# Two gates' rows by transposes, a sum and a round trip through DRAM instead of products with ones

## The chip, the cores and the metric

The kernel runs on one core of a Trainium2 chip. The core has a matrix engine (TensorE, "PE" in the profile, with its weight loads as "PEld"), a vector engine (VectorE, "DVE"), an activation engine (ScalarE, "ACT"), a general engine (GpSimd, "POOL") and SyncE ("SP"), which here only issues transfers. Sixteen DMA engines carry the transfers that SP, ACT and POOL issue. PE writes to eight PSUM banks; ACT and DVE read them.

The metric is the device time of one execution in microseconds. Three runs of the kernel before took 773.56 to 774.21 us, with a median of 773.87.

## The reference

One transformer block for 2048 tokens of width 640, all in float32. A condition vector `c` modulates it: six rows of 640 come from one product, and two of them, `ga` and `gb`, are the gates that this case is about.

```python
mod = (_silu(c) @ w_mod).reshape(c.shape[0], 6, 1, -1)
sa, ca, ga, sb, cb, gb = (mod[:, 0], mod[:, 1], ..., mod[:, 5])
h = _layernorm(x) * (1 + ca) + sa
x = x + ga * _A_ref(h, A_wqkv, A_w_phi, A_wo)     # linear attention, 32 heads of 20
h = _layernorm(x) * (1 + cb) + sb
x = x + gb * _B_ref(h, B_w1, B_b1, B_w2, B_b2)    # two layers, relu squared, width 1728
```

In `_A_ref`, q and k pass a product per head and two softmaxes, one of the values and one of the negated values; the features then give `num / den` of linear attention, and `wo` projects the result.

A gate is a row along the feature axis, and the kernel needs it spread over all 128 partitions: `ga` is multiplied into `wo` when the weights are prepared, `gb` into the second layer's results and its bias.

## The kernel before, in words

**Tiles.** Tokens are cut into 16 tiles of 128 (`NT`); x is loaded in pairs of tiles (`XB[j]`, j = 0 to 7). The 640 features are cut into five chunks of 128 (`NC`). Every weight and activation is split into a high and a low part, and a product is three matmuls (`three`). Most matmuls come from one line, L77 in `mm`, so the profile tells them apart by the tile that they write: `pk`, `pq`, `pv` for the projections, `kvp` for keys times values, `pwo` for the output projection, `up` and `acc` for the two layers.

**The modulation.** The rows `sa` and `ca` (parts 0 and 1) are made at the start. For parts 2 to 5, `mod_mac` and `gb_mac` load a piece of `w_mod` of 128 rows (`stage`, on SP) and accumulate it on DVE, each partition with its own entry of silu(c) (`mac`, L293 and L295). What is left in `MA[part]` is 128 partial rows, which must be summed over the partitions. There are two ways in the code:

- Parts 3 and 4, which are needed as columns: `mod_turn` transposes chunks of `MA` on PE (L304) into a PSUM bank, ACT copies them into a row `mt` (L305), and `mod_sum` sums along the free axis on DVE (L309). Four chunks go together after a `do_kv`, the fifth rides in the bank of a LayerNorm transpose, in `t1(..., more=...)`.
- Parts 2 and 5, the gates, which are needed as rows on all partitions: `mod_row` multiplies by a 128 x 128 matrix of ones on PE (L327), 320 columns at a time, and ACT copies the result into `ga_b` or `gb_b` (L328).

**Phase 1** (L711 to L758) goes over the tiles t = 2 to 13: the key projection, the value projection, `do_kv` for the two tiles before (at even t), the LayerNorm of a coming pair of x tiles (`ln_parts`, in three parts: the sums, the squares, the scaling), then the query projection with the transposes `t1` of the next pair within it. PE's order is written out by hand. DVE, ACT, POOL and SP are ordered by the planner, which simulates the work with its own costs and keeps the order of the code as priority; `tc.issue_after(x)` adds that an instruction comes behind x on its engine, and `newest(engine)` is the last one written so far. The LayerNorm of the last pair (j = 7) has its sums and squares at t = 11 (`NT - 5`), the sums behind the copy of that tile's key projection.

`SIDE[t]` at the end of a tile holds the modulation's accumulation and the preparation of `wo` (`prep_wo`: load, times `ga_b` at L498, split); `AFTER_KV[t]` stands behind `do_kv`, and `LAST_COL[t]` says which part's fifth chunk rides along.

**Phase 2** starts at L761. There PE, DVE, ACT and POOL have a hand-written order, and SP is still the planner's. The last keys and values are done, `kv_diags` turns the sums of keys times values (`kvt`, L834 and L835), and `num(j)`, `num_hi(j)`, `num_lo(j)` make the numerators: products `numa`, `numb`, `numc`, copies of their high part by ACT (L942), a product with a negated unit matrix that leaves the low part (L948), and its copy (L951). `tr_e` transposes the scaled query features (`te`, copied to `ept`). Then a loop over j = 0 to 7 does the output projection (`do_wo`) and the next pair's transposes and numerators. At j = 5 it makes `bb`, the gated bias, from `gb_b` (L1139).

**Phase 3** from L1506 on is the two layers.

**Buffers.** A tile has a tag, and a tag has so many buffers: the rows `s1` have five (pieces of `w_mod`, the turned rows `mt`, raw `wo`, raw weights of the layers); the PSUM tag `tp` has one bank and serves `t1`, `mod_turn` and `mod_row` in phase 1; the projections' tag `pj` has four; the banks of phase 2 (`bank`) are three. Whoever wants a buffer waits until all readers of its previous tile are done.

Of the kernel before, what the change touches and what calls it, by code (L numbers as in the profile page):

```python
# [15 lines left out]
P = 128  # L16
# [34 lines left out]
def kernel(  # L51
# [85 lines left out]
    def tp(name):  # L137
        return psA.tile([P, 512], F32, tag="tp", name=name)
# [160 lines left out]
    def mod_turn(part, p, *cs_):  # L299
        t = MT.setdefault(part, None) or row("s1", f"mt{part}")  # L300
        MT[part] = t
        a, n = cs_[0] * P, len(cs_) * P
        for i, c in enumerate(cs_):
            nc.tensor.transpose(p[:, i * P : (i + 1) * P], MA[part][:, c * P : (c + 1) * P], ident)  # L304
        nc.scalar.activation(t[:, a : a + n], p[:, :n], AF.Copy)  # L305
# [12 lines left out]
    def mod_mac(part, *ks):  # L318
        for k, t in [(k, stage(part * D, k)) for k in ks]:
            with tc.issue_after(newest(ET_.DVE)):  # L320
                mac(t, t, k, MA.get(part))
            MA[part] = t

    def mod_row(part, dest, h, p=None):
        p = p or tp(f"mr{part}_{h}")
        c = slice(h * HALF, (h + 1) * HALF)
        nc.tensor.matmul(p[:, :HALF], ones, MA[part][:, c], start=True, stop=True)  # L327
        nc.scalar.activation(dest[:, c], p[:, :HALF], AF.Copy)  # L328

    def ln_parts(xt, nm, spare=None):  # L330
        sm = small([P, 2], "sm", f"sm{nm}")
# [45 lines left out]
    def newest(engine):  # L377
        return next(i for i in reversed(nc.cur_bb.bb.instructions) if i.engine == engine)
# [55 lines left out]
    def exps(e):  # L434
        nc.scalar.activation(e[:, 0], e[:, 0], AF.Exp)  # L435
        nc.scalar.activation(e[:, 1], e[:, 1], AF.Exp, scale=-1.0)  # L436
# [86 lines left out]
    def wo_weights(*gs):  # L523
# [1 line left out]
            prep_wo(g, ga_b)  # L525

    AFTER_KV = {
        6: lambda: mod_turn(3, tp("mc3"), 0, 1, 2, 3),
        8: lambda: mod_row(2, ga_b, 0),
        10: lambda: mod_turn(4, tp("mc4"), 0, 1, 2, 3),  # L530
        12: lambda: t1(NT // 2 - 1, 2, 3),
    }
    LAST_COL = {7: (3, cols_b[:, 0:5]), 11: (4, cols_b[:, 5:10])}
    SIDE = {
        2: lambda: mod_mac(3, 0, 1, 2),
        3: lambda: (mod_mac(3, 3, 4), mod_mac(4, 0)),
        4: lambda: mod_mac(4, 1, 2),
        5: lambda: (mod_mac(4, 3, 4), mod_mac(2, 0)),
        6: lambda: mod_mac(2, 1, 2, 3),
        7: lambda: mod_mac(2, 4),  # L540
        8: lambda: None,
        9: lambda: wo_weights(0, 1),
        10: lambda: wo_weights(2),
        11: lambda: None,
# [166 lines left out]
    for t in range(2, NT - 2):  # L711
        j, i = divmod(t, 2)
        if i == 0 and j < NT // 2 - 2:
            load_x(j + 2)
        PK[t] = row("s2", f"k{t}")
        to_sb(proj("k", t), PK[t])
        if t == NT - 4:
            t1(j + 1, 0, 1)
        if t == 9:
            mod_row(2, ga_b, 1)  # L720
        norm = j + 1 if i == 0 and t < NT - 4 else j + 2 if t == NT - 5 else None
        if norm:
            parts = ln_parts(XB[norm], f"a{norm}")
            with tc.issue_after(newest(ET_.Activation)):
                next(parts)
        p = proj("v", t, (1, 0, lambda: t1(j + 1, 4)) if t == NT - 3 else None)
        if i == 0:
            do_kv(t - 2)
            do_kv(t - 1)
            if t in AFTER_KV:  # L730
                AFTER_KV[t]()
        v_out(t, p)
        if norm:
            next(parts)
        EK[t] = tok2("k", f"ek{t}")
        spread(PK[t], EK[t], f"k{t}")
        exps(EK[t])
        if norm and not i:
            next(parts)
        if i and t < NT - 4:  # L740
            t1(j + 1, 2, 3)
        with tc.issue_after(newest(ET_.DVE)):
            k_norm(EK[t], t)
        if t < NT - POSTPONED:
            do_q(t, (1, 3, lambda: t1(j + 1, 4, more=LAST_COL.get(t))) if i else None)
            if norm and i:
                with tc.issue_after(newest(ET_.Activation)), tc.issue_after(DONE[0]):
                    next(parts)
            if i:
                with tc.issue_after(DONE[1]):  # L750
                    q_chain(t)
            else:
                q_chain(t)
        if i == 0 and t < NT - 4:
            t1(j + 1, 0, 1)
        SIDE[t]()
    pe.__exit__(None, None, None)
    behind.close()  # L758
# [40 lines left out]
    def bank(nm):  # L799
        return psB.tile([P, 512], F32, tag="m", name=nm)  # L800
# [30 lines left out]
    def kv_diags():  # L831
        kvt[:] = [bank(f"kvt{b}") for b in range(2)]
        for g in range(5):
            nc.tensor.transpose(kvt[g // 4][:120, (g % 4) * P : (g % 4) * P + P], kvs[:, 120 * g : 120 * g + 120], ident)  # L834
        nc.tensor.transpose(kvt[1][:80, P : P + 40], kvs[:40, 600:680], ident[:40, :40])  # L835

    def kv_out():
        for b, (g0, g1) in enumerate(((0, 4), (4, 5))):
# [266 lines left out]
    load_e(4)  # L1105
    do_q(q0 + 3, (1, 8, lambda: tr_e(0, range(3))))
    tr_e(0, range(3, NG))
    mod_row(5, gb_b, 0, bank("mr5_0"))
    num(0)
    num_hi(0)  # L1110
    mod_row(5, gb_b, 1, bank("mr5_1"))
    num_lo(0)
    e_prod(3)
    e_recip(2)
# [8 lines left out]
    for j in range(NB):  # L1123
# [61 lines left out]
            do_wo(j, 1, 1, 11, 16)  # L1185
        if j in SPREAD:
            exps(EQ[KEPT + SPREAD[j]])
        load_e(c + 2)
        if j == 5:
            next(ln0)  # L1190
# [474 lines left out]
```

## Time and profile before

| | us |
|---|---|
| median of 3 runs (lowest to highest) | 773.87 (773.56 to 774.21) |
| the profiled execution | 773.97 |
| its span, first to last instruction | 772.2 |
| PE busy | 764.6 |
| DVE busy | 580.3 |
| ACT busy | 443.3 |
| POOL busy | 145.5 |

The page of a profile covers one execution. Matmuls are pipelined, so a record of a matmul lasts longer than the distance to the next one: what a group of matmuls costs is read from the chain that ended last, where each piece begins when the one before it lets go. That chain is followed back from the last instruction: at each step to what released it, or else to the instruction before it on its engine. In the timeline, a bracket behind a row gives the idle time of the engine before it and who ended it. A share of busy time is a mean over stages with different limits, so a place is judged by its own rows.

### The profile page before, as it was taken

The numbers are of one execution on the slowest core, as the hardware profiler recorded it, in microseconds if no ns is written. First come the engines' busy times: TensorE is split into PE (matmuls) and PEld (weight loads), VectorE is DVE, ScalarE is ACT, GpSimd is POOL, SyncE is SP. The second block draws the span as 40 slices with busy tenths as digits, with TensorE's granted clock in tenths as the row PEclk, the third lists the DMA queues.
The fourth block names the chain that finished last, engine by engine and source line by source line (L and its number), as shares of the span: only waits on it lengthen the run. The fifth ranks groups of instructions, "written<-read, shape, count | busy, mean of one in ns | idle before, by whom it ended". The sixth has DMA issues, their size and how long they took to land.

```text
span 772.2 us, 15334 instructions
## 1 busy us (share of the span) xinstructions
PE 764.6 (99%) x5989; PEld 744.1 (96%) x5989; DVE 580.3 (75%) x1057; ACT 443.3 (57%) x995; POOL 145.5 (19%) x301
## 2 busy tenths in 40 slices
PE   9999999999999999999999999999999999999997
PEld 9999999999999979998999999999999999999997
DVE  6598897968999899976266666767767566685666
ACT  5766756667853355656776647456463645546331
POOL 3001101202000255631001001122221313213110
PEclk9999999999999999999999999999999999999999
DMA  9711431512333354232247465997666758667460
GB/s 332 297 65 73 137 103 54 186 37 101 133 103 109 111 160 157 86 105 101 91 137 251 137 212 215 292 320 234 202 178 213 231 178 264 198 185 208 128 171 35
DMA packets 50552, 126.03 MB, mean 163 GB/s; under 512 B 5992, under 2 KB 6760, under 8 KB 50480
## 3 DMA queue, kind: packets, MB, share of 16 engines
q1 hardware_dynamic: 33144, 83.99, 31.7%
q0 software_dynamic: 14752, 35.76, 16.7%
q10 hardware_dynamic: 2583, 5.30, 1.8%
q8 instruction: 47, 0.77, 0.4%
q14 instruction: 26, 0.20, 0.1%
HBM read 95.05 MB, written 29.88 MB: 162 GB/s over the span
## 4 chain that ended last, share of the span: by engine, by line
PE 94%; ACT 2%; DVE 1%; DMA 1%; issue 1%; POOL 0%; SPq 0%; ACTq 0%; POOLq 0%
PE up L77 24%; PE acc L77 17%; PE pwo L77 10%; PE pk L77 8%; PE pq L77 8%; PE pv L77 8%; PE acc3x L77 5%; PE kvp L449 2%; PE te L913 2%; PE tb L356 1%; PE numa L77 1%; PE numb L77 1%; PE numc L77 1%; PE ta L356 1%; PE foldk L279 1%; PE foldq L279 1%
## 5 line engine op out<-in xcount | busy, mean ns | idle before, releaser
L77 PE MATMUL up<-h,w 128*128 128x256 f32 x1640 | 206.5, 278 | 0.2 <-ACT ft L1235 0.2
L77 PEld LDWEIGHTS up<-h,w 128*128 128x128 f32 x1640 | 196.1, 188 | 0.3 <-ACT ft L1235 0.3
L1235 ACT ACTIVATE ft<-up,b_t 128x256 f32<-128x256 f32 x104 | 48.8, 469 | 113.9 <-PE up L77 113.4
L77 PE MATMUL acc<-w,ra 128*128 128x384 f32 x452 | 97.9, 335 | 0.0
L1236 DVE TENSOR_TENSOR ft<-ft 128x256 f32<-128x256 f32 x104 | 44.0, 424 | 50.9 <-ACT ft L1235 49.2
L77 PE MATMUL pwo<-wo,ot 128*128 128x256 f32 (+3 forms) x512 | 81.3, 312 | 0.0
L77 PEld LDWEIGHTS pwo<-wo,ot 128*128 128x128 f32 (+1 forms) x512 | 74.9, 188 | 3.0 <-issue 2.7
L77 PE MATMUL pq<-wq,hT 128*128 128x384 f32 (+1 forms) x480 | 75.4, 312 | 0.0
L77 PEld LDWEIGHTS acc<-w,ra 128*128 128x128 f32 x452 | 72.6, 188 | 0.7 <-DVE ra L87 0.5
L77 PE MATMUL pk<-wk,hT 128*128 128x384 f32 (+1 forms) x480 | 72.7, 308 | 0.0
L77 PEld LDWEIGHTS pq<-wq,hT 128*128 128x128 f32 x480 | 71.2, 188 | 0.8 <-issue 0.2
L77 PE MATMUL pv<-wv,hT 128*128 128x384 f32 (+1 forms) x480 | 71.8, 307 | 0.0
L77 PEld LDWEIGHTS pk<-wk,hT 128*128 128x128 f32 x480 | 70.5, 188 | 0.4 <-issue 0.2
L77 PEld LDWEIGHTS pv<-wv,hT 128*128 128x128 f32 x480 | 70.0, 188 | 0.2
L87 DVE TENSOR_TENSOR ra<-ft,ra 128x384 fp32r<-128x384 f32 (+2 forms) x86 | 36.8, 449 | 32.9 <-ACT ra L1259 20.2
L77 PE MATMUL acc3x<-w,ra 128*128 128x256 f32 x248 | 42.4, 278 | 0.0
L1259 ACT ACTIVATE ra<-ft 128x384 fp32r<-128x384 f32 x48 | 25.2, 525 | 28.4 <-DVE ft L1236 22.4
L1345 POOL DMA_DIRECT2D ring_a<-td_a x34 | 18.2, 536 | 123.6 <-PE acc L77 99.6
L77 PEld LDWEIGHTS acc3x<-w,ra 128*128 128x128 f32 x248 | 39.8, 188 | 0.2 <-DVE ra L87 0.2
L1250 DVE TENSOR_TENSOR ft<-ft 128x128 f32<-128x128 f32 x136 | 33.3, 285 | 1.2
L440 DVE TENSOR_REDUCE sk<-ek 128x64 f32<-128x1280 f32 x16 | 23.7, 1483 | 13.9 <-ACT ek L435 13.4
L477 DVE TENSOR_REDUCE rs_q<-eq 128x64 f32<-128x1280 f32 x16 | 23.7, 1479 | 9.6 <-ACT eq L436 9.6
(260 smaller groups left out, 1413.7 us busy)
## 6 DMA issues: line engine op xcount, KB each, us to landing
ring_c<-td_c POOLq DMA_DIRECT2D x34, 384.0 KB, 4.0
ring_a<-td_a POOLq DMA_DIRECT2D x34, 384.0 KB, 3.9
ring_b<-td_b POOLq DMA_DIRECT2D x34, 256.0 KB, 3.9
esp<-eq SPq DMA_DIRECT2D x12, 640.0 KB, 3.1
el<-esp SPq DMA_DIRECT2D x12, 640.0 KB, 5.0
rw<-in_w SPq DMA_DIRECT2D x23, 320.0 KB, 3.6
wm<-in_w_mod SPq DMA_DIRECT2D x20, 320.0 KB, 3.4
xb<-in_x SPq DMA_DIRECT2D x8, 640.0 KB, 4.0
```

The source lines that it names most:

```text
L77: nc.tensor.matmul(o, a, b, start=first and i == 0, stop=last and i == len(terms) - 1, skip_group_check=skip,)
L87: (eng or nc.vector).tensor_tensor(out_lo, full, hi.bitcast(F32), op=ALU.subtract)
L279: nc.tensor.matmul(p[g // 3][:, (g % 3) * 120 : (g % 3) * 120 + n], r, bd_t[:120, g * 120 : g * 120 + n], start=True, stop=True,)
L356: nc.tensor.transpose(p[:, i * P : (i + 1) * P], xn[:, i, d * P : (d + 1) * P], ident)
L440: nc.vector.tensor_reduce(s, heads(flat(e)), axis=AX.X, op=ALU.add)
L449: nc.tensor.matmul(kvp[g // 4][64 * c : 64 * c + 64, a : a + 2 * n].rearrange("p (s n) -> p s n", s=2), v[:, u], e[:, :, o : o + n], start ...
L477: nc.vector.tensor_reduce(s, heads(flat(e)), axis=AX.X, op=ALU.add)
L1235: nc.scalar.activation(r, p, AF.Relu, bias=b1_t[:, f : f + 1])
L1236: nc.vector.tensor_tensor(r, r, r, op=ALU.mult)
L1250: nc.vector.tensor_tensor(t[:, o], t[:, a], t[:, b], op=op)
L1259: nc.scalar.activation(a[:, 0, :3], t[:, :3], AF.Copy)
L1345: nc.gpsimd.dma_start(RING[j, n, r], TD[n][r].bitcast(F32R))
```

## The change

Both gates now go the way of parts 3 and 4, with one more step. Their `MA` is transposed in chunks, ACT copies the chunks, DVE sums them into a column per chunk (`gate_a`, `gate_b`: 128 x 5), and the new `spread_row` writes these columns to a row in DRAM and reads that row back into all 128 partitions, with two transfers on SP.

Phase 1 takes part 2 first, then 3, then 4, where it took 3, 4, 2. At t = 6 stand the transposes of part 2, at t = 8 those of part 3, at t = 10 those of part 4, as before; the fifth chunks are at t = 7, 9 and 11. `spread_row` for `ga_b` stands in `SIDE[7]`. In phase 2 the five transposes of part 5 stand in `kv_diags`, the first in the free half of a bank that is there already and four in a bank of their own, and both `mod_row` calls around `num(0)` go. The sum of part 5 and the spread of `gb_b` stand at the end of the loop's j = 3.

Apart from that, the sums of the last pair's LayerNorm are written at the end of t = 10 (`NT - 6`), behind the newest instruction of ACT there, and no longer at t = 11; its squares stand at t = 11 where the sums stood, and the scaling stays.

```diff
-    def mod_row(part, dest, h, p=None):
-        p = p or tp(f"mr{part}_{h}")
-        c = slice(h * HALF, (h + 1) * HALF)
-        nc.tensor.matmul(p[:, :HALF], ones, MA[part][:, c], start=True, stop=True)
-        nc.scalar.activation(dest[:, c], p[:, :HALF], AF.Copy)
+    GD = [dram.tile([NC, P], F32, name=f"gate{h}") for h in range(2)]
+
+    def spread_row(h, col, dest):
+        nc.sync.dma_start(GD[h].rearrange("c p -> p c"), col)
+        nc.sync.dma_start(dest, GD[h].rearrange("c p -> (c p)")[None, :].to_broadcast([P, D]))
...
     AFTER_KV = {
-        6: lambda: mod_turn(3, tp("mc3"), 0, 1, 2, 3),
-        8: lambda: mod_row(2, ga_b, 0),
+        6: lambda: mod_turn(2, tp("mc2"), 0, 1, 2, 3),
+        8: lambda: mod_turn(3, tp("mc3"), 0, 1, 2, 3),
         10: lambda: mod_turn(4, tp("mc4"), 0, 1, 2, 3),
         12: lambda: t1(NT // 2 - 1, 2, 3),
     }
-    LAST_COL = {7: (3, cols_b[:, 0:5]), 11: (4, cols_b[:, 5:10])}
+    gate_a = const.tile([P, NC], F32, name="gate_a")
+    gate_b = const.tile([P, NC], F32, name="gate_b")
+    LAST_COL = {7: (2, gate_a), 9: (3, cols_b[:, 0:5]), 11: (4, cols_b[:, 5:10])}
     SIDE = {
-        2: lambda: mod_mac(3, 0, 1, 2),
-        3: lambda: (mod_mac(3, 3, 4), mod_mac(4, 0)),
-        4: lambda: mod_mac(4, 1, 2),
-        5: lambda: (mod_mac(4, 3, 4), mod_mac(2, 0)),
-        6: lambda: mod_mac(2, 1, 2, 3),
-        7: lambda: mod_mac(2, 4),
-        8: lambda: None,
+        2: lambda: mod_mac(2, 0, 1, 2),
+        3: lambda: (mod_mac(2, 3, 4), mod_mac(3, 0)),
+        4: lambda: mod_mac(3, 1, 2),
+        5: lambda: (mod_mac(3, 3, 4), mod_mac(4, 0)),
+        6: lambda: mod_mac(4, 1, 2),
+        7: lambda: (spread_row(0, gate_a, ga_b), mod_mac(4, 3)),
+        8: lambda: mod_mac(4, 4),
         9: lambda: wo_weights(0, 1),
...
-        if t == 9:
-            mod_row(2, ga_b, 1)
         norm = j + 1 if i == 0 and t < NT - 4 else j + 2 if t == NT - 5 else None
         if norm:
-            parts = ln_parts(XB[norm], f"a{norm}")
+            if not i:
+                parts = ln_parts(XB[norm], f"a{norm}")
             with tc.issue_after(newest(ET_.Activation)):
                 next(parts)
...
         v_out(t, p)
-        if norm:
+        if norm and not i:
             next(parts)
...
         if i == 0 and t < NT - 4:
             t1(j + 1, 0, 1)
+        if t == NT - 6:
+            parts = ln_parts(XB[j + 2], f"a{j + 2}")
+            with tc.issue_after(newest(ET_.Activation)):
+                next(parts)
         SIDE[t]()
...
         nc.tensor.transpose(kvt[1][:80, P : P + 40], kvs[:40, 600:680], ident[:40, :40])
+        mod_turn(5, kvt[1][:, 2 * P :], 4)
+        mod_turn(5, bank("mc5"), 0, 1, 2, 3)
...
     tr_e(0, range(3, NG))
-    mod_row(5, gb_b, 0, bank("mr5_0"))
     num(0)
     num_hi(0)
-    mod_row(5, gb_b, 1, bank("mr5_1"))
     num_lo(0)
...
+        if j == 3:
+            mod_sum(5, gate_b)
+            spread_row(1, gate_b, gb_b)
         load_e(c + 2)
```

## The prediction

> **What bounds the kernel now.** I read the page's first part, then the waits of TensorE, then the chain that ended last with the timelines of the places that the change touches. The page first (columns: busy time, share of the span, instructions), then the waits of PE, longest first (PE, line, whom it waited for: total, times, longest; the two left out are shorter still).
>
> ```profile
> span 772.2 us, 15334 instructions
> PE 764.6 (99%) x5989; PEld 744.1 (96%) x5989; DVE 580.3 (75%) x1057; ACT 443.3 (57%) x995; POOL 145.5 (19%) x301
> ```
>
> ```profile
> PE warm L623 <- POOL bdc L154: 1.1, 1, 1.1
> PE ta L356 <- ACT hfa L367: 0.6, 1, 0.6
> ...
> ```
>
> TensorE is the bound, and its longest wait belongs to the start. So the time moves by what the change takes from or adds to PE's own stream, by the one wait of 0.6 us on `ta`, and by waits that it creates. The profiled execution took 773.97 us (span 772.2 and 1.77 around it), 0.10 above the median of the runs, 773.87; the sum goes against 773.97.
>
> **First gate (part 2), phase 1.** Chain rows (start, length, what) with the transposes of a part at t = 6 (`mc`), the fifth transpose riding in `ta` at t = 7, and the two products with ones (`mr`) at t = 8 and 9:
>
> ```profile
> 123.24 0.58 PE mc L304 x4
> 123.82 4.38 PE pq L77 x30
> ...
> 141.09 0.11 PE ta L304
> ...
> 153.67 0.77 PE mr L327 x2
> 154.44 4.32 PE pq L77 x30
> ...
> 163.57 0.54 PE mr L327 x2
> ```
>
> The parts run 2, 3, 4 instead of 3, 4, 2, so t = 6 keeps four transposes. At t = 8 four transposes replace `mr`: with the `pq` behind each, 0.58 + 4.38 = 4.96 for 0.77 + 4.32 = 5.09, 0.13 less. At t = 9 `mr` goes (0.54) and one transpose comes (0.11). Together 0.56 us off PE. Bounds: 0.4, if the lone transpose costs a start of its own like the 0.58 of four (0.15 over 4 x 0.11), to 0.56; no reading of these rows gives more. From the tiles' views (line, operation, count: shortest, median and longest ns, first and last start):
>
> ```profile
> L304 PE MATMUL mc<-ident,wm x8: 272/272/328, 123.2 to 184.9; 128*128 128x128 f32 x8
> L328 ACT ACTIVATE ga_b<-mr x2: 416/424/431, 157.3 to 166.4; 128x320 f32<-128x320 f32 x2
> L305 ACT ACTIVATE mt<-mc x2: 573/574/575, 125.7 to 188.7; 128x512 f32<-128x512 f32 x2
> L309 DVE TENSOR_REDUCE cols_b<-mt x2: 808/814/819, 144.3 to 206.5; 128x5 f32<-128x640 f32 x2
> L498 DVE TENSOR_TENSOR rwo<-rwo,ga_b x6: 812/818/820, 182.6 to 231.1; 128x640 f32<-128x640 f32 x5, 120x640 f32<-120x640 f32 x1
> ```
>
> The first row's 272 ns is a record's length; four of them took 0.58 us, so the starts lie about 0.11 apart. The Trainium skill (TensorE: Matmul & The Clock Gate, Part 4) gives a PE transpose some 275 ns in a kernel's context and speaks against the change: ten at that price come to 2.75 us. The record's length agrees, the spacing does not; by that rule the sum below would be an estimated 773.3 and not 771.8.
>
> The rest of the first gate lies beside PE. ACT loses two copies of 0.42 and gains one of 0.57 and one of a quarter of its columns; DVE gains one sum of 0.81 (part 3's, now at t = 9). A tile lasts some 15 us (153.67 less 123.24, halved), and PE asks neither for a result, so I take nothing for either. If DVE has no slack there, the sum delays what ACT waits for by its 0.81. The gate's row now goes through SP: a write of 640 single floats, then a broadcast load of 320 KB that waits for the write. SP stands until the sum (about 145 by the 144.3 of the row above), then until the write has landed; behind it stand the loads of `wo`, of x and of the next w_mod pieces, and the EQ stores. The nearest row for the two transfers, the stored tiles' reload (KB, median us to landing), and SP's issue of the last x tile:
>
> ```profile
> el<-esp SPq DMA_DIRECT2D x12, 640.0 KB, 5.0
> 172.16 0.38 SPq L221 DMA_DIRECT2D xb<-in_x  x1
> ```
>
> At 5 us each `ga_b` stands at 155, and its first user starts at 182.6: a cover of 27 us beyond the two transfers. I take nothing; a loss begins only where the round trip passes 37 us, and a gain is excluded, since the products with `ga_b` are queued behind t = 9's work on DVE. The Trainium skill (DMA: Bandwidth & Descriptors, Rules for kernel authors) says that a last dimension that is not contiguous becomes one descriptor per element: 640 here. No row of this trace shows such a write, and the sum would be the same by it while those take less than the cover.
>
> **LayerNorm of x tile 7.** Chain at t = 11, the PE timeline's row that waits, and ACT's and DVE's timelines (idle time before an instruction and its releaser in brackets):
>
> ```profile
> 196.12 1.43 ACT xb L336 x4
> ...
> 198.19 0.62 ACT eq L436
> ```
>
> ```profile
> 202.78 0.44 PE L356 MATMUL ta<-ident,xb 128*128 128x128 f32 x2 [0.62 <-ACT hfa L367]
> ```
>
> ```profile
> 192.72 0.49 ACT L425 ACTIVATE k<-pk 128x384 f32<-128x384 f32 x1 [0.61 <-PE pk L77]
> 195.11 0.74 ACT L435 ACTIVATE eq<-eq 128x640 f32<-128x640 f32 x1 [1.90 <-DVE eq L432]
> ```
>
> ```profile
> 196.40 0.82 DVE L432 TENSOR_TENSOR eq<-q,mxq 128x640 f32<-128x640 f32 x1
> ```
>
> The two sums with their accumulator reads (1.43 on ACT, and POOL's L337) move from behind t = 11's key copy to behind t = 10's last `hT` copy. There ACT sits idle 0.61 + 1.90 = 2.51 us, which holds 1.43; the key copy at 192.72 may start some 0.8 later, and its products have four PSUM buffers. x tile 7 is issued at 172.16, 20 us before. Then the `eq` exponential (198.19) is limited by DVE's 196.40 + 0.82 = 197.22, so ACT's queue gains 0.97 ahead of the `hfa` that PE waits for: more than 0.62. I take the whole 0.62; ends 0 and 0.62. The squares and POOL's three small operations stay behind the key copy and come earlier with it, no later. Next late would be nothing that PE's waits show.
>
> **Last gate (part 5), start of phase 2.** Chain from the first product with ones to the first product of the output projection; ACT's copy of numc's high part; the same stage at j = 1, without `mr`; the transposes of the block that the new ones join:
>
> ```profile
> 261.30 0.55 PE kvt L834 x5
> ...
> 270.75 0.81 PE mr L327 x2
> 271.55 0.61 PE numa L77 x4
> ...
> 274.62 0.73 PE mr L327 x2
> 275.36 0.24 PE numa L948
> ...
> 275.82 0.24 PE numc L948 x2
> 276.07 7.63 PE pwo L77 x48
> ...
> 286.28 1.08 PE numa L77 x8
> ...
> 289.10 1.45 PE pwo L77 x11
> ```
>
> ```profile
> 274.67 0.66 ACT L942 ACTIVATE ot<-numc 128x256 fp32r<-128x256 f32 x2 [0.27 <-PE numc L77]
> ```
>
> Before: 276.07 - 270.75 = 5.32 us. After: the products take what they take at j = 1, 289.10 - 286.28 = 2.82 (the 0.25 that j = 0 has more stands beside `mr`'s extra bank, which goes). Then the second `mr` is missing as cover: ACT's copies of numc end 274.67 + 0.66 = 275.33, 0.71 after numc's products (274.62), and PE has only 275.82 - 275.36 = 0.46 of work before it needs them. So a new wait of 0.25, then 0.25 for numc: 2.82 + 0.46 + 0.25 + 0.25 = 3.78, 1.54 less. Ends: 1.79 without the wait, 1.08 if PE waits the whole 0.71. I take 1.54, since both halves of it are rows of this place. Against it five more transposes in `kv_diags`: 0.55 like the five at 261.30 (0.73 if all cost like the four at 123.24). Net 0.99 less; ends 0.35 and 1.24.
>
> Beside PE: ACT copies the turned row (0.57 and the quarter) ahead of `kv_out`, whose tiles PE reads only after 270.75, nine us behind the transposes; it loses 2 x 0.42 at 272 to 276. DVE's sum and the row's round trip come at j = 3, ahead of a DVE gap of 3.34 us, and `gb_b` is first read at 354.5. DVE's chain does not move while PE starts the projection about 1 us sooner; its least slack is the last scaling for j = 1's second transposes, done at 291.08 + 1.41 = 292.49 and read from 294.44 on: 1.95, about 1 left. The rows, from PE's and DVE's timelines and the view of `gb_b`:
>
> ```profile
> 294.44 1.47 PE L913 MATMUL te<-ident,ezb 128*120 128x128 f32 x12
> ```
>
> ```profile
> 291.08 1.41 DVE L893 TENSOR_TENSOR ezb<-el,dn 128x1200 f32<-128x1200 f32 x1
> ...
> 340.64 1.49 DVE L477 TENSOR_REDUCE rs_q<-eq 128x64 f32<-128x1280 f32 x1 [3.34 <-ACT eq L436]
> ```
>
> ```profile
> L1139 DVE TENSOR_TENSOR bb<-b2s,gb_b x1: 816/816/816, 354.5 to 354.5; 128x640 f32<-128x640 f32 x1
> ```
>
> **Sum.** 773.97 - 0.56 - 0.62 - 0.99 = 771.80 us, 0.28% less. All later work is PE's own stream, so the gain is kept to the end.
>
> **Rivals.**
> - *The LayerNorm's wait stays.* ACT, DVE, POOL and SP are ordered by the planner in phase 1, and it plans anew; if the sums land elsewhere, or the sum of part 3 at t = 9 (0.81 on DVE) pushes what ACT waits for, PE waits as before: 771.80 + 0.62 = 772.42, up to 773.2 with the added 0.81. For it: the chain's rows there (196.12 on) are ACT's, so PE follows whatever ACT is given to do. Against: the idle 2.51 us.
> - *A transpose costs its record.* Ten at 0.272 are 2.72 where I count 0.58 + 0.11 + 0.55 = 1.24: 1.48 more, 773.3. For it: nothing but the record. Against: the spacing in three rows.
> - *The copy of part 3 finds no buffer.* This is the one that ends slower. The rows `s1` are five, and part 2's and 5's turned rows are new users. The first of these timeline rows (POOL, DVE, PE) shows that POOL's clearing for a `wo` row takes a buffer the moment a turned row's sum lets go of it:
>
> ```profile
> 145.27 0.63 POOL L488 MEMSET rwo<- 128x640 f32 x1 [3.37 <-DVE cols_b L309]
> 152.63 0.88 DVE L295 SCALAR_TENSOR_TENSOR wm<-wm,cs,wm 128x640 f32<-128x640 f32 x1
> 158.59 0.60 PE L356 MATMUL ta<-ident,xb 128*128 128x128 f32 x4
> ```
>
> If that happens again, the sum of part 3, two w_mod pieces and two `wo` rows hold all five when the copy of t = 8's transposes wants one. The next comes free with part 4's last product, now a tile after 152.63, at about 167.8 (15.2 later); the bank `tp` is single, and PE's next transposes at 158.59 wait until 167.8 + 0.88 + 0.57 = 169.3, 10.7 us: 782.5. It decides from a delay of 3.7 us on. Against it: the copy stands ahead of those `wo` rows in the code.
>
> **How the numbers follow.** Chances: forecast 0.60, the wait stays 0.20, full-length transposes 0.04, no buffer 0.11, other new stalls of such size 0.05. A measurement tells about 0.2%, 1.55 us, from no change: faster is below 772.3, slower above 775.4. The forecast's own range goes from its large ends (0.56, 0.62, 1.24: 771.55, less 0.3 for half the spread of the runs, 773.56 to 774.21) to its small ones for the gates (0.4, 0.62, 0.35): 771.2 to 772.6, of which I put 0.05 above 772.3. So faster is 0.55, same 0.05 + 0.20 + 0.04 = 0.29, slower 0.16. The range for 8 in 10 is 771.1 to 774.0; it takes in the first two rivals and leaves out the slow cases.
>
> **What the profile after would show.** No `mr`; `mc` at t = 6, 8, 10 and a second group of five beside `kvt`; PE's wait on `hfa` at t = 11 gone or under 0.1; a wait of PE of about 0.25 on ACT `ot` ahead of numc's L948; `ga_b` landed long before its first product. Wrong would be: any PE wait over 0.5 us in 120 to 215, DVE's scaled tiles late at j = 1, or SP's loads behind the gate's row late.

## The result, and the profile after

The changed kernel took 771.49 us (median of six runs, 770.97 to 771.88), beside 773.76 us for the kernel before on the same chip (six runs, 773.54 to 774.21). The ratio is 0.997, with a 95% interval from 0.9957 to 0.9982: 2.27 us, or 0.3%, faster. The prediction was 771.80 us in a range of 771.1 to 774.0. The profiled execution took 771.32 us.

The first part of the page of the changed kernel (busy time, share of the span, instructions), and the waits of TensorE (total, times, longest), all of them:

```profile
span 769.6 us, 15344 instructions
PE 763.2 (99%) x5991; PEld 744.3 (97%) x5991; DVE 582.6 (76%) x1059; ACT 444.2 (58%) x995; POOL 143.9 (19%) x301
```

```profile
PE warm L625 <- POOL bdc L154: 1.1, 1, 1.1
PE up L77 <- ACT ft L1243: 0.2, 1, 0.2
```

PE is still the bound. The wait on `hfa` at t = 11 is gone, and none over 0.5 us came.

Where the time went is read by cutting both profiled spans at the same instructions of PE's stream. These rows of PE's timeline start the stages in the changed kernel (start, length, line, operation):

```profile
150.46 1.79 PE L449 MATMUL kvp<-ek,vt 128*64 128x120 f32 x30
...
180.84 2.40 PE L449 MATMUL kvp<-ek,vt 128*64 128x120 f32 x42
...
259.11 0.71 PE L839 MATMUL kvt<-ident,kvs 128*120 128x128 f32 x5
...
273.07 4.11 PE L77 MATMUL pwo<-wo,ot 128*128 128x384 f32 x26
...
280.49 2.69 PE L920 MATMUL te<-ident,ezb 128*120 128x128 f32 x22
```

The same rows of the kernel before:

```profile
151.11 1.14 PE L449 MATMUL kvp<-ek,vt 128*64 128x120 f32 x18
...
182.04 1.14 PE L449 MATMUL kvp<-ek,vt 128*64 128x120 f32 x18
...
261.13 0.71 PE L834 MATMUL kvt<-ident,kvs 128*120 128x128 f32 x5
...
275.90 1.26 PE L77 MATMUL pwo<-wo,ot 128*128 128x384 f32 x5
...
283.52 0.71 PE L913 MATMUL te<-ident,ezb 128*120 128x128 f32 x5
```

| stretch (us) | before | after | difference | predicted |
|---|---|---|---|---|
| start to t = 8's first `kvp` | 151.11 | 150.46 | -0.65 | 0 |
| t = 8's first `kvp` to t = 10's: the first gate | 30.93 | 30.38 | -0.55 | -0.56 |
| t = 10's first `kvp` to the first `kvt`: LayerNorm's wait | 79.09 | 78.27 | -0.82 | -0.62 |
| first `kvt` to first `pwo`: the last gate | 14.77 | 13.96 | -0.81 | -0.99 for both |
| first `pwo` to the next `te` | 7.62 | 7.42 | -0.20 | |
| from there to the span's end | 488.68 | 489.11 | +0.43 | 0 |
| span | 772.2 | 769.6 | -2.6 | -2.17 |

The four middle rows make 2.38 us, and the medians differ by 2.27. The first and last rows aren't the change's: the start lies between 11.76 and 12.68 us (PE's first product with `raw_q`) over all the kernels below, whatever they change, and the stretch of the last row between 488.64 and 489.24 us.

### The profile page after: what moved, and what is told of

It reads as the page before. It is cut to its first block, busy times and chain, and to the rows that moved or that the text cites. A ratio compares the mean times of both kernels' runs of the same rounds, so it can differ in the third digit from the quotient of the medians.

```text
span 769.6 us, 15344 instructions
## 1 busy us (share of the span) xinstructions
PE 763.2 (99%) x5991; PEld 744.3 (97%) x5991; DVE 582.6 (76%) x1059; ACT 444.2 (58%) x995; POOL 143.9 (19%) x301
## 2 busy tenths in 40 slices
DMA packets 52152, 126.69 MB, mean 165 GB/s; under 512 B 7336, under 2 KB 8104, under 8 KB 52080
## 4 chain that ended last, share of the span: by engine, by line
PE 98%; ACT 1%; DVE 0%; POOL 0%; issue 0%; POOLq 0%
PE up L77 24%; PE acc L77 17%; PE pwo L77 10%; PE pq L77 9%; PE pk L77 9%; PE pv L77 9%; PE acc3x L77 5%; PE kvp L449 3%; PE te L920 2%; PE tb L356 1%; PE numa L77 1%; PE numc L77 1%; PE foldk L279 1%; PE numb L77 1%; PE ta L356 1%; PE foldq L279 1%
## 5 line engine op out<-in xcount | busy, mean ns | idle before, releaser
L440 DVE TENSOR_REDUCE sk<-ek 128x64 f32<-128x1280 f32 x16 | 23.7, 1484 | 12.8 <-ACT ek L435 11.3
```

What stands on the lines that cost most here:

```text
L440: nc.vector.tensor_reduce(s, heads(flat(e)), axis=AX.X, op=ALU.add)
```

## The experiments

All ratios are to the kernel before on the same chip, whose median was 773.62 to 773.98 us over these runs. By their intervals a single median is sure to 0.7 to 1 us only, so the parts are read from the stages of the traces; the table at the end of this section has those of nine kernels.

**The first gate alone.** The kernel before with part 2 first, its transposes, sum and DRAM row; the last gate and the LayerNorm as before (the lines undone in the changed kernel):

```diff
-        mod_turn(5, kvt[1][:, 2 * P :], 4)
-        mod_turn(5, bank("mc5"), 0, 1, 2, 3)
...
+    mod_row(5, gb_b, 0, bank("mr5_0"))
     num(0)
     num_hi(0)
+    mod_row(5, gb_b, 1, bank("mr5_1"))
...
-        if t == NT - 6:
-            parts = ln_parts(XB[j + 2], f"a{j + 2}")
...
```

> The kernel before with the first gate alone done the new way (parts 2, 3, 4 in that order, its row by transposes, sum and DRAM); LayerNorm and last gate as before. By the sum of the prediction: PE's stream loses 0.56 us between t = 8 and t = 9, the wait at t = 11 on ACT stays or not as the planner has it; time 0.5 to 0.6 below before, 1.2 to 1.4 if the wait goes too. Rival (the planner's new order, not the LayerNorm, took the wait away): the PE wait on hfa at t = 11 is gone here already.

Measured: 772.67 us, ratio 0.9983 (0.9975 to 0.9992). The gain is 1.14 us by the medians. In the trace it is 0.56 in the first gate's stage and 0.82 between t = 10 and `kvt`, less 0.21 in the two stretches behind: PE's wait at t = 11 is gone although the LayerNorm is written as before.

**The LayerNorm edit alone.**

```diff
         if norm:
-            parts = ln_parts(XB[norm], f"a{norm}")
+            if not i:
+                parts = ln_parts(XB[norm], f"a{norm}")
...
+        if t == NT - 6:
+            parts = ln_parts(XB[j + 2], f"a{j + 2}")
...
```

> The kernel before with the LayerNorm's edit alone. By the prediction: the wait of 0.62 us on hfa at t = 11 is gone and the time is 0.6 to 0.8 lower. Rival (the planner's new order did it): the wait stays, time within 0.2 of before.

Measured: 772.94 us, 0.9989 (0.998 to 0.9997), 0.87 us by the medians. The stretch behind t = 10 loses 0.77 us and the wait goes, so this edit is also enough by itself.

**The last gate alone.** Part 5's transposes, sum and DRAM row in the kernel before; phase 1 untouched.

```diff
+        mod_turn(5, kvt[1][:, 2 * P :], 4)
+        mod_turn(5, bank("mc5"), 0, 1, 2, 3)
...
-    mod_row(5, gb_b, 0, bank("mr5_0"))
     num(0)
     num_hi(0)
-    mod_row(5, gb_b, 1, bank("mr5_1"))
...
+        if j == 3:
+            mod_sum(5, gate_b)
+            spread_row(1, gate_b, gb_b)
```

> The kernel before with the last gate alone done the new way. By the prediction: 1.0 us lower (1.54 less around num(0), 0.55 more in kv_diags); by the trace after, where PE waits about 0.5 instead of 0.25 for the copies of numc: 0.8 lower. Rival (the gain in the trace after stands elsewhere, in start and planner): under 0.4 lower.

Measured: 772.46 us, 0.9983 (0.9975 to 0.9992). The two stages of phase 2 are 0.76 and 0.22 us shorter. Phase 1 keeps its wait, in this row of PE's waits:

```profile
PE ta L362 <- ACT hfa L373: 0.6, 1, 0.6
```

The stretch from t = 10 to `kvt` is 0.38 us longer than before in this trace (79.47 for 79.09), though nothing was edited there: such a stretch can differ by some tenths between two kernels without an edit in it.

**The changed kernel without the LayerNorm edit.** The diff of the second experiment, taken back out of the changed kernel.

```diff
-        if t == NT - 6:
-            parts = ln_parts(XB[j + 2], f"a{j + 2}")
...
```

> The changed kernel without its LayerNorm edit. By the prediction: PE waits 0.6 us or more on hfa at t = 11 again and the time is 0.6 to 0.8 above the changed kernel, 1.5 below before. Rival (the planner's new order took the wait away): as fast as the changed kernel, 2.2 below before.

Measured: 771.46 us, 0.9963 (0.995 to 0.9977), which is the changed kernel's time. With both gates moved, the LayerNorm edit is worth nothing: the stretch behind t = 10 is 78.27 us with it and without it. The three single gains, 1.14 + 0.87 + 1.35, make 3.36 us; the 0.82 of the wait is in the first and in the second, and without one of them 2.54 is left, near the 2.27 of the whole.

**A cover for the new wait in the last gate.** Four of part 5's transposes move between the numerators' high copies and the products that leave the low parts.

```diff
-        mod_turn(5, bank("mc5"), 0, 1, 2, 3)
...
     num_hi(0)
+    mc5 = bank("mc5")
+    for i in range(4):
+        nc.tensor.transpose(mc5[:, i * P : (i + 1) * P], MA[5][:, i * P : (i + 1) * P], ident)
     num_lo(0)
+    nc.scalar.activation(MT[5][:, : 4 * P], mc5, AF.Copy)
```

> The changed kernel, with four of part 5's transposes moved from kv_diags to the place between num_hi(0) and num_lo(0), where the second product with ones stood; their copy on ACT comes behind num_lo's. If the missing cover is what PE waits for there (0.5 us), the transposes fill it: 0.4 to 0.5 below the changed kernel. Rival (what PE loses there is a restart and not the wait on the copies): nothing below it, within 0.1.

Measured: 771.22 us, 0.9964 (0.9951 to 0.9976), the changed kernel's time within the interval. The chain that ended last, of this kernel (start, length, what):

```profile
272.62 0.23 PE numc L954 x2
272.86 7.69 PE pwo L77 x48
```

`numc`'s negated products take 0.23 now, for 0.51 in the changed kernel (below), so `pwo` starts 0.32 us earlier, counted from `kvt`. But `pwo` runs 7.69 for 7.44, and 0.26 is back by the next `te`. ACT's three low copies follow one another behind its high copies, and `pwo` reads them. By ACT's timelines they end 14.97 us after `kvt` here and 15.04 in the changed kernel, so they hardly came sooner: the loss of PE taken away ahead of ACT's chain seems to return behind it, in stops too short for the list of waits.

**Four times the transposes at t = 8.**

```diff
-    def mod_turn(part, p, *cs_):
+    def mod_turn(part, p, *cs_, times=1):
...
-        for i, c in enumerate(cs_):
+        for i, c in times * list(enumerate(cs_)):
...
-        8: lambda: mod_turn(3, tp("mc3"), 0, 1, 2, 3),
+        8: lambda: mod_turn(3, tp("mc3"), 0, 1, 2, 3, times=4),
```

> The changed kernel with the four transposes of t = 8 written four times over the same bank, twelve more; the result is the same. If a transpose costs its spacing of 0.11: 1.3 us above the changed kernel. If it costs its record of 0.272: 3.3 above.

Measured: 772.47 us, 0.998 (0.9971 to 0.9989), 0.98 above the changed kernel by the medians. The chain of this kernel, with one row for the sixteen:

```profile
152.82 1.90 PE mc L304 x16
```

In the changed kernel four take 0.59, so twelve more cost 1.31 in this row, and 1.28 us in the whole stage: 0.107 each. The rival by which each costs its record (0.272) would be 3.3 us, and neither the stage nor the medians show that.

**The gate's row later, by the order of the code.** `spread_row(0, ...)` moves from `SIDE[7]` to `SIDE[9]`.

```diff
-        7: lambda: (spread_row(0, gate_a, ga_b), mod_mac(4, 3)),
+        7: lambda: mod_mac(4, 3),
...
-        9: lambda: wo_weights(0, 1),
+        9: lambda: (spread_row(0, gate_a, ga_b), wo_weights(0, 1)),
```

> The changed kernel with the first gate's write and read in DRAM moved from the end of t = 7 to the end of t = 9, just ahead of the weights that are multiplied by it: its cover is gone. The trace after has 15 us from the write's issue to the row's landing (143.8 to 155.1 to 159). If that round trip has a price once it is not covered: DVE stands for several us at the first product with ga_b, and PE for a part of it, some 2 to 8 us above the changed kernel. Rival (wo's weights are needed only in phase 2, the planner goes round it): within 0.3 of the changed kernel.

Measured: 771.17 us, 0.9963 (0.9951 to 0.9976). The edit missed what it was for: the planner issued the write at 143.81 us, as in the changed kernel. Nothing follows for the cover.

**The gate's row later, held on SP.** The same move, with the two transfers ordered behind SP's newest instruction there.

```diff
+    def late_row():
+        with tc.issue_after(newest(ET_.SP)):
+            spread_row(0, gate_a, ga_b)
...
-        9: lambda: wo_weights(0, 1),
+        9: lambda: (late_row(), wo_weights(0, 1)),
```

> The changed kernel with the first gate's write and broadcast load held on the SP queue behind the store of t = 9's eq (issue about 183, for 143.8), so that the cover of the DRAM round trip is gone: about 15 us of round trip (11.3 to the read's issue, 3.9 to its landing) put ga_b at about 198, while VectorE's queue wants it at about 184.4 for the first wo product. Theory (the cover is what makes the round trip free): VectorE stands about 14 us in front of that product with the low parts of hT for t = 11 behind it, TensorE stops for them, and the time rises by 5 to 12 us, to 776 to 783. Rival (phase 1 has slack on VectorE for it, since wo is needed in phase 2 only): TensorE loses under 1 us, 771.5 to 772.5.

Measured: 781.08 us, 1.0094 (1.008 to 1.0107): 9.6 us slower than the changed kernel. From the timelines of SP, DVE and PE of this kernel:

```profile
180.22 0.43 SPq L327 DMA_DIRECT2D gate<-gate_a  x1
190.57 0.32 SPq L328 DMA_DIRECT2D ga_b<-gate  x1
190.98 15.12 SPq L490 DMA_DIRECT2D rwo<-in_wo  x6
```

```profile
196.19 0.83 DVE L498 TENSOR_TENSOR rwo<-rwo,ga_b 128x640 f32<-128x640 f32 x1 [12.29 <-DMA rwo<-in_wo]
```

```profile
198.22 6.39 PE L77 MATMUL pv<-wv,hT 128*128 128x384 f32 x30 [4.97 <-ACT q L425]
```

SP stands 10.35 us for the write, with the loads of `wo` from the third row on queued behind it; DVE then stands 12.29 us in front of its first product with `ga_b`, ACT behind DVE, and PE behind ACT's copy of q. The bracket names a load of `wo`, but by SP's timeline those of the first two rows were issued from 153.34 to 163.83. What the first product lacked by the order of the code is `ga_b`, whose read was issued 0.41 us ahead of the load that is named; its landing isn't recorded. So the round trip is free in the changed kernel because it starts early.

**The gate's row written in whole runs.** This kernel leaves out the right order of the gate's 640 entries: the column goes to DRAM as 128 runs of five floats, not as 640 single ones.

```diff
-    GD = [dram.tile([NC, P], F32, name=f"gate{h}") for h in range(2)]
+    GD = [dram.tile([P, NC], F32, name=f"gate{h}") for h in range(2)]
...
-        nc.sync.dma_start(GD[h].rearrange("c p -> p c"), col)
-        nc.sync.dma_start(dest, GD[h].rearrange("c p -> (c p)")[None, :].to_broadcast([P, D]))
+        nc.sync.dma_start(GD[h], col)
+        nc.sync.dma_start(dest, GD[h].rearrange("p c -> (p c)")[None, :].to_broadcast([P, D]))
```

> The changed kernel with the gates' columns written to DRAM in the order in which they lie (128 runs of five floats in place of 640 single floats), and read back in that order; what it leaves out is putting the gate's 640 entries in their right order. If the single floats make the write long: the time from the write's issue to the read's issue falls from 11.3 us to 2 to 5. Rival (it is the wait for another thing on SP, or what every write to DRAM takes): it stays at 10 or more. The kernel's time stays within 0.3 of the changed kernel by both, since the round trip is covered.

Measured: 771.49 us, 0.9965 (0.9951 to 0.9979), no change of the time. SP's timeline of this kernel, and then of the changed one; the read waits for the write, so the distance of the two rows is the write's:

```profile
143.90 0.33 SPq L327 DMA_DIRECT2D gate<-gate_a  x1
146.03 0.33 SPq L328 DMA_DIRECT2D ga_b<-gate  x1
```

```profile
143.75 0.38 SPq L327 DMA_DIRECT2D gate<-gate_a  x1
155.09 0.34 SPq L328 DMA_DIRECT2D ga_b<-gate  x1
```

2.13 us for 11.34: single floats cost 9 us more in this pair of traces (the first gate's write took 9.3 to 11.3 us in the kernels that have it), and the cover hides them.

**What GpSimd has to do with t = 11.** With the LayerNorm edit out of the account, why does the first gate's edit take the wait away? The three small GpSimd operations of x pair 6's LayerNorm differ. They feed the scaling on ACT, and behind it come the exponentials of t = 10, DVE's work on them, and the `hfa` that PE waited for at t = 11. POOL's timelines, of the kernel before and of the changed one:

```profile
182.62 0.83 POOL L342 TENSOR_SCALAR sqa<-sqa 128x2 f32<-128x2 f32 x1 [2.66 <-ACT junka L341]
183.54 1.30 POOL L343 TENSOR_TENSOR sqa<-sqa,mhalf 128x2 f32<-128x2 f32 x1
184.92 0.88 POOL L344 TENSOR_TENSOR nba<-sma,sqa 128x2 f32<-128x2 f32 x1
```

```profile
181.42 0.60 POOL L342 TENSOR_SCALAR sqa<-sqa 128x2 f32<-128x2 f32 x1 [2.65 <-ACT junka L341]
182.11 0.71 POOL L343 TENSOR_TENSOR sqa<-sqa,mhalf 128x2 f32<-128x2 f32 x1
182.89 0.24 POOL L344 TENSOR_TENSOR nba<-sma,sqa 128x2 f32<-128x2 f32 x1
```

They end 3.76 us after t = 10's first `kvp` before (185.80 less 182.04) and 2.29 after it now (183.13 less 180.84). Beside them ran DVE, before and then after:

```profile
182.59 0.82 DVE L498 TENSOR_TENSOR rwo<-rwo,ga_b 128x640 f32<-128x640 f32 x1
183.45 1.56 DVE L432 TENSOR_TENSOR ek<-k,mxk 128x640 f32<-128x640 f32 x2
```

```profile
181.16 0.82 DVE L498 TENSOR_TENSOR rwo<-rwo,ga_b 128x640 f32<-128x640 f32 x1
182.25 1.56 DVE L432 TENSOR_TENSOR ek<-k,mxk 128x640 f32<-128x640 f32 x2 [0.28 <-PE kvp L449]
```

The same DVE products stand there, but the first is 1.43 us earlier where POOL's first operation is 1.20 earlier, and in both kernels that operation ends with the product beside it (183.45 and 183.41 before, 182.02 and 181.98 after). Behind it DVE ran on before, and idled 0.28 us after. So POOL's second operation began 0.09 us behind the `ek` products before, and 0.14 ahead of them after. It then ran on beside them in both: for 1.30 us before, and for 0.71 after. Three kernels test whether DVE stretches POOL's operations, and whether this makes the wait.

The first takes the `wo` products of t = 9 away from that place in the kernel before:

```diff
-        9: lambda: wo_weights(0, 1),
-        10: lambda: wo_weights(2),
+        9: lambda: None,
+        10: lambda: wo_weights(0, 1, 2),
```

> The kernel before with one edit: the first two rows of wo are scaled at t = 10 and not at t = 9, so VectorE has no wo product beside the three small GpSimd operations of x pair 6's LayerNorm (L342 to L344). Theory (those three are stretched by VectorE's instructions running back to back, and by them PE's wait at t = 11 arises): they take about 0.6, 0.7 and 0.24 us as in the changed kernel, not 0.83, 1.30 and 0.88; PE's wait on hfa at t = 11 falls from 0.6 to under 0.1; from t = 10's first kvp to z about 71.4 us for 72.17; time 773.98 - 0.8 = 773.2. Rival 1 (the planner's order of ScalarE alone makes the wait): the three keep 0.8, 1.3 and 0.9, the wait stays 0.6, 774.0. Rival 2 (the wait is VectorE's own load): the wait goes, but the three keep their lengths.

Measured: 773.56 us, ratio 1.0 (0.9991 to 1.0008). POOL's three take 0.19, 0.71 and 0.64, and PE's wait on `hfa` is gone. But the time stays, since PE has a new wait, on the low part of `hT`, behind the `wo` products that now stand on DVE ahead of it (a row of PE's waits):

```profile
PE pk L77 <- DVE hT L87: 0.5, 1, 0.5
```

The second adds one DVE instruction to the changed kernel without the LayerNorm edit, at the place where DVE idled:

```diff
+    def extra():
+        with tc.issue_after(newest(ET_.DVE)):
+            nc.vector.tensor_scalar(ga_b, ga_b, 1.0, None, op0=ALU.mult)
...
-        9: lambda: wo_weights(0, 1),
+        9: lambda: (extra(), wo_weights(0, 1)),
```

> The changed kernel without the LayerNorm edit, with one VectorE instruction more at t = 9 (the gate's row times 1.0, 128 x 640, about 0.55 us), between the sums of eq and the first wo product, where VectorE had 0.28 us idle beside the three small GpSimd operations. Theory (VectorE running back to back stretches GpSimd's small operations): the three take 0.8, 1.3 and 0.9 us again, not 0.60, 0.71 and 0.24, and PE's wait at t = 11 is back with 0.3 to 0.6; time 771.5 + 0.5 = 772.0. Rival 1 (VectorE doesn't touch GpSimd): the three keep 0.60, 0.71 and 0.24; a wait, if any, is at most the 0.27 by which VectorE's next product starts later; 771.5 to 771.8.

Measured: 771.92 us, 0.9972 (0.9962 to 0.9982), 0.46 us above the same kernel without the instruction. The second and third of POOL's operations, from its timeline:

```profile
182.09 1.35 POOL L343 TENSOR_TENSOR sqa<-sqa,mhalf 128x2 f32<-128x2 f32 x1
183.52 0.88 POOL L344 TENSOR_TENSOR nba<-sma,sqa 128x2 f32<-128x2 f32 x1
```

They are as long as in the kernel before. The first took 0.26: beside it ran the added one-input instruction, and it was over before the product of row 0 began. The stage behind t = 10 is 0.77 us longer, but no wait on `hfa` is back: 0.34 of it lies in the `pk` of t = 11 (4.65 us to the next `ta`, for 4.31) and the rest is spread, in stops too short for the list of waits. The added instruction's own 0.48 us on DVE may be part of it, so the price of the stretch isn't separated from it.

The third moves the two `wo` rows in the kernel before to t = 11, where nothing stood:

```diff
-        9: lambda: wo_weights(0, 1),
+        9: lambda: None,
...
-        11: lambda: None,
+        11: lambda: wo_weights(0, 1),
```

> The kernel before with the first two rows of wo scaled at t = 11 (where nothing stood) and not at t = 9, so that their four VectorE products are neither beside the small GpSimd operations of x pair 6 nor ahead of hT's low parts at t = 11. Theory (before, PE's loss at t = 11 is VectorE's wo rows: they stretch GpSimd's three operations, and moved by one tile only they stand ahead of hT instead): the three take 0.2 to 0.6, 0.7 and 0.2 to 0.65 us, PE waits neither on hfa nor on hT, from t = 10's first kvp to z 71.35 to 71.6 us for 72.17, time 773.62 - 0.7 = 772.9. Rival (another limit stands right behind, whatever is moved): 72.0 or more in that stage, 773.5 to 774.

Measured: 773.93 us, 1.0003 (0.9994 to 1.0012). POOL's three take 0.19, 0.71 and 0.65, and PE passes t = 11 without a wait, on `hfa` or on `hT`. The stretch behind t = 10 gains only 0.19 all the same: 0.72 at t = 11, less 0.42 in a later `kvp`, which waits 0.23 for DVE's `ek`, and 0.11 behind it. The time lacks more than that, and ahead of the moved products: from PE's first product with `raw_q` to t = 8 this kernel takes 139.05 us where the others take 138.44 to 138.66, and from t = 8 to 10 it loses 0.26, with a wait of PE of 0.20 on DVE's `wm`. No product was moved there; the planner may have ordered it anew, which isn't shown. So the rival's time held (its stage of 72.0 or more all but: 71.98), but this run can't tell what the products cost at t = 11. At t = 10 they weren't free: the wait on `hT` is seen.

Together: that DVE's products stretch POOL's operations is shown from both sides. That the first gate's edit takes PE's wait away by this alone isn't: the stretch and DVE's own load were never changed apart, so its share of the 0.82 stays open.

Stage lengths of these kernels (us, from the starts in PE's timeline as in the first table; the runs' medians):

| kernel | t = 8 to 10 | t = 10 to `kvt` | `kvt` to `pwo` | `pwo` to `te` | POOL's three | median |
|---|---|---|---|---|---|---|
| before | 30.93 | 79.09 | 14.77 | 7.62 | 0.83, 1.30, 0.88 | 773.76 |
| changed | 30.38 | 78.27 | 13.96 | 7.42 | 0.60, 0.71, 0.24 | 771.49 |
| first gate alone | 30.37 | 78.27 | 14.83 | 7.77 | 0.60, 0.71, 0.24 | 772.67 |
| LayerNorm alone | 30.87 | 78.32 | 14.77 | 7.63 | 0.81, 1.33, 0.88 | 772.94 |
| last gate alone | 31.06 | 79.47 | 14.01 | 7.40 | 0.76, 1.38, 0.88 | 772.46 |
| both gates, no LayerNorm edit | 30.37 | 78.27 | 13.96 | 7.42 | 0.60, 0.71, 0.24 | 771.46 |
| the same, one DVE instruction more | 30.37 | 79.04 | 13.97 | 7.44 | 0.26, 1.35, 0.88 | 771.92 |
| before, `wo` rows to t = 10 | 30.97 | 79.13 | 14.79 | 7.64 | 0.19, 0.71, 0.64 | 773.56 |
| before, `wo` rows to t = 11 | 31.19 | 78.90 | 14.84 | 7.64 | 0.19, 0.71, 0.65 | 773.93 |

## Why the prediction was right, point by point

**The first gate: right.** 0.56 was counted; 0.55 was measured in the changed kernel, and 0.56 in the two others that have this edit with or without the last gate. The chain of the changed kernel:

```profile
153.00 0.59 PE mc L304 x4
...
170.82 0.11 PE ta L304
```

Four transposes cost 0.59 and the lone one 0.11, as taken; the bound that gave the lone one a start of its own is out, and so is the rival that prices a transpose by its record. The Trainium skill (TensorE: Matmul & The Clock Gate, Part 4) has some 275 ns for one, of bf16 data where these are float32; the trace agrees as to the record and not as to the price, 0.107 us over twelve more.

**The LayerNorm term: the wait went, but not by this edit alone, and its size was 0.2 too small.** The step "I take the whole 0.62" counted the gain to the moved sums. The edit alone does give it (0.77 of the 0.82). But the first gate's edit gives it too, and with that one in the kernel the sums' move adds nothing (771.46 without it, 771.49 with it). What failed is the step that treated the two edits as separate terms: both end the same wait. A row of the kernel before that the prediction didn't weigh, POOL's three operations of 3.01 us together, lay on the chain that ended last, ahead of that wait, and told that ACT's idle time of 2.51 us wasn't the only lever (the first and the last of the three in that chain of the kernel before):

```profile
182.62 0.84 POOL sqa L342
...
184.92 0.89 POOL nba L344
```

That the first gate's edit would reach the same wait was foreseen nowhere. In so far it is luck that the term came true: it would have with the sums left where they were.

The rival "the wait stays" had the planner's new order in view as a risk; here the first gate's new order took the wait away.

The size is 0.82 and not 0.62: PE's bracket holds only the idle time, and without the stop the `ta` starts before the record ahead of it has ended (at 200.81, with that record running to 200.97). From the start of `pq` to the `ta` that waited, 18 matmuls and the wait took 3.88 us before and 3.06 after (200.81 less 197.75), by these rows of PE's timelines, before and after:

```profile
198.90 3.26 PE L77 MATMUL pq<-wq,hT 128*128 128x384 f32 x18
```

```profile
197.75 3.22 PE L77 MATMUL pq<-wq,hT 128*128 128x384 f32 x18
200.81 0.38 PE L356 MATMUL ta<-ident,xb 128*128 128x128 f32 x2
```

**The last gate: the sum came out, by luck in part; two of its parts were off.** Predicted 0.99, measured 0.81 up to `pwo`, which is as far as the prediction's sum goes, and 0.20 behind it. The chain of the changed kernel:

```profile
259.98 0.26 PE kvt L304
260.24 0.44 PE mc L304 x4
260.67 5.23 PE pq L77 x38
...
269.15 1.09 PE numa L77 x8
...
271.10 0.89 PE numc L77 x8
...
272.01 0.67 ACT ot L949 x2
...
272.72 0.51 PE numc L955 x2
273.23 7.44 PE pwo L77 x48
```

- The products: 2.84 for 2.82 (from 269.15 to 271.99).
- The copies of `numc`'s high part hold PE from 271.99 to 272.72, 0.73 for the 0.46 + 0.25 of the prediction. The new stop is there, with its size; PE's waits don't list it, since only 0.09 us of it is idle time between records (272.63 to 272.72).
- `numc`'s two products after it took 0.51, not 0.25: the mis-sized term. With 0.02 more in each of the two rows above, 4.08 from `numa` to `pwo` stand against 3.78, so 1.24 went and not 1.54. The row before had them without a stop, and the kernel with the cover, which has none there either, shows 0.23. So the stop cost more than its wait, as at t = 11.
- The five transposes cost 0.26 + 0.44 = 0.70, near the upper end of 0.73 and not the 0.55 taken; the chance was there in the row of four at 123.24.
- Against these 0.45 us (0.30 and 0.15) stand two gains counted at nothing, which is the luck in the sum: 0.26 between the transposes and the first product of the numerators (270.75 less 262.01 before, by the row below, and 269.15 less 260.67 after), and 0.20 from `pwo` to the next `te`. The second fits the removed copy of `mr` by ACT at 275.40, ahead of the low copies that `pwo` reads; it comes with the last gate in the kernels that have it, the one with the cover aside (7.40 to 7.45 for 7.62 to 7.77), but the copy wasn't taken away alone. For the first no run shows the cause.

The chain of the kernel before, behind its last `kvt`:

```profile
262.01 5.44 PE pq L77 x38
```

So "it loses 2 x 0.42 at 272 to 276", put down as beside PE, may have been a term of the sum.

**What was counted as covered stayed covered.** The write took 11.34 us and not the 5 assumed, the load's landing 3.9: `ga_b` stands at 159, first used at 181.16, and 22 us are left. The kernel that holds the row on SP shows the price once that is gone: 9.6 us. The prediction's bound of 37 us wasn't tried at its edge. DVE's last scaling for j = 1's second transposes had 1.95 us of slack before and, by these rows of DVE's and PE's timelines, 1.02 now, for the predicted 1:

```profile
289.07 1.41 DVE L900 TENSOR_TENSOR ezb<-el,dn 128x1200 f32<-128x1200 f32 x1
```

```profile
291.50 1.48 PE L920 MATMUL te<-ident,ezb 128*120 128x128 f32 x12
```

**The slow rival** (the copy of part 3 finds no buffer) didn't come: the copy ran 1.7 us behind its transposes, and it was POOL's clearing of the second `wo` row that stood 9.91 us for a buffer, with no wait of PE behind it (POOL's timeline of the changed kernel):

```profile
163.14 0.63 POOL L488 MEMSET rwo<- 128x640 f32 x1 [9.91 <-DVE wm L295]
```

No run shows the rival's price.

## What to carry to other kernels

Two edits that end the same wait are one term of a sum, not two: before adding them, follow the wait's chain back over every engine, small operations included, and ask whether the other edit already moves a link of it. A wait removed ahead of an engine's chain of copies can come back behind it, and the same work moved by a tile can move the loss and not the time, so a place is safe only where the moved work's own followers have slack. A slow step is free while it starts early enough: read how far its first user lies behind it, and how many other transfers queue behind its wait.

## What the runs showed of the hardware that wasn't expected

- GpSimd's three operations on 128 x 2 elements in x pair 6's LayerNorm took 0.19, 0.71 and 0.24 us at their shortest, and up to 0.83, 1.38 and 0.88 beside VectorE's two-input products. One added DVE instruction stretched the last two again, and with the products moved away the three took 0.19, 0.71 and 0.64. Running beside a product isn't enough: the 0.71 of the changed kernel began 0.14 us ahead of one and wasn't stretched. Nor is 0.88 the most: for x pair 5 the last of the three took 2.17 us in the kernel before (POOL's timeline, from 152.86 to 155.03), beside a run of VectorE's operations with two such products at its end (until 154.98). The Trainium skill (SBUF — State Buffer, Who interferes with whom) says that a DVE instruction with two SBUF inputs contends with a GpSimd instruction that reads SBUF, and that issue order decides who blocks. The trace agrees, with an operation of 0.19 that takes 0.83 and ends 0.04 us behind the product beside it, and with the 0.71 that began first.
- A write of 640 single floats to DRAM took 9.3 to 11.4 us until the read that waited for it was issued, the same bytes in 128 runs 2.1 us at the first gate and 2.7 at the last. The Trainium skill (DMA: Bandwidth & Descriptors, Rules for kernel authors) has one descriptor per element for such a transfer. The trace agrees in the count: the kernel with whole runs moved 1025 packets under 512 bytes fewer (6311 for 7336), where two writes of 128 in place of 640 make 1024. The time is from the runs.
